# The pitch of V's rows in a cached-attention kernel: 320 bytes instead of 258

## The chip, the cores and the metric

The kernel runs on one core of one Trainium2 chip. The metric is the time of one execution on the device in microseconds (us); lower is better. The time before was 189.4 us, the median of three runs (189.28 to 189.42). All runs in this document are in the fast state (the clock is not held back), with a granted TensorE clock of 0.997 to 1.000 of full speed.

The profile names the engines PE (matmuls of TensorE), PEld (weight loads of TensorE), DVE (VectorE), ACT (ScalarE), POOL (GpSimd) and SP (SyncE, which issues most of the DMA transfers). SBUF is the on-chip memory in which the tiles lie.

## The reference, cut to what matters

```
B, Sq, D = 8, 32, 1024
Hq, Hkv, Sk, Dh = 32, 4, 8192, 128        # W = 2048 keys are used
q = (x @ wq)                              # to heads
k = k_cache[:, :, Sk - W:, :]             # each K/V head serves 8 query heads
v = v_cache[:, :, Sk - W:, :]
p = softmax(q @ k.T * Dh ** -0.5)
out = (p @ v) @ wo
```

There are 8 × 4 = 32 units, one for each batch row and K/V head. A unit has 2048 keys, cut into 16 blocks of 128, and 8 heads × 32 = 256 queries.

## The kernel before

For each unit the kernel makes scores with keys on the partitions (K is the stationary operand), takes the exponential on ACT without a maximum, and multiplies the result, P, by V; these last matmuls are called PV below. V gets a column of ones, so that the softmax sum comes out as column 129 of the same matmul. A landing buffer is a tile into which a DMA load writes. The parts that matter here:

```
self.VW = self.Dh + 1                                                     # 129
self.va = [self.c1.tile([P, self.KT, self.VW], BF16, name=f"va{i}") for i in range(3)]
# ... after it, in the same part of SBUF, lie the landing buffers of wq, wo, K and V
def va_copy(self, ui):                    # once per unit, on DVE
    self.nc.vector.tensor_copy(out=self.va[ui % 3][:, :, 0:self.Dh], in_=self.v_sb[ui][:, :, :])

for c in range(NCH):                      # 4 chunks of 4 key blocks in a unit
    for jj in range(CJ):                  # scores: 4 matmuls of 256 columns
        nc.tensor.matmul(s_ps[:, jj, :], lhsT=self.kT[ui][:, c * CJ + jj, :], rhs=q_u, ...)
    nc.scalar.activation(out=pT[:, :, :], in_=s_ps[:, :, :], func=ACT.Exp, ...)
    def pv(...):                          # run two chunks later: 8 matmuls of 129 columns
        for jj in range(CJ):
            j = c * CJ + jj
            for qt in range(QT_N):        # two halves of the queries
                nc.tensor.matmul(o_ps[:, qt, 0:self.VW], lhsT=pT[:, jj, qt * P:(qt + 1) * P], rhs=va[:, j, :], ...)
    # ... pieces of the projections and K transposes fill the rest of the slot
```

So the moving operand of PV is row j of `va`, 129 bf16 elements at j × 258 bytes, streamed twice in a row. In "a group of four rows" below, a group is one chunk: eight PV matmuls, rows 0, 0, 1, 1, 2, 2, 3, 3, preceded by the score matmuls in 126 of the 128 groups.

## Time and profile before

| | before |
|---|---|
| time, median of 3 | 189.4 us |
| PE busy | 181.3 us, 96% |
| ACT, DVE, POOL busy | 70%, 61%, 50% |
| mean step of PV matmuls (start to next start) | 57.9 ns |
| load rate between 12 and 27 us | 409 GB/s |

The page of the profile, part 1 (busy time of each engine) and the three PV groups of part 5 (busy us, mean ns of one, idle time before):

```profile
PE 181.3 (96%) x2048; PEld 154.5 (82%) x2064; DVE 115.2 (61%) x267; ACT 131.9 (70%) x133; POOL 94.2 (50%) x150
...
L473 PE MATMUL o_ps<-va_112,pT 128*128 128x129 bf16 x352 | 27.5, 220 | 0.0
L473 PE MATMUL o_ps<-va_113,pT 128*128 128x129 bf16 x352 | 27.3, 220 | 0.1
L473 PE MATMUL o_ps<-va_114,pT 128*128 128x129 bf16 x320 | 25.0, 220 | 0.0
```

PV keeps TensorE for 27.5 + 27.3 + 25.0 = 79.8 us. The 220 ns of one matmul say little: matmuls overlap (the next one starts 57.9 ns later on average), and what counts is the time from one start to the next. Those steps are not a line of any view; they are differences of the start times in the trace's matmul records. The start times of the eight PV matmuls of one group near 95 us, in us, and the steps between them in ns:

```
before: row      0       0       1       1       2       2       3       3
start        95.073  95.130  95.187  95.247  95.303  95.363  95.419  95.478
step to next     57      57      60      56      60      56      59      56
```

The first row has even steps of 57 ns; in rows 1, 2 and 3 the step after the first streaming is 59 to 61 ns, 384 times in the trace (12 rows × 32 units) without exception.

The view of waits (engine, line and tile, released by what: us in total, times, longest), the lines that matter:

```profile
ACT pT L464 <- PE s_ps L462: 35.5, 99, 1.2
...
PEld L462 <- POOL kTv L255: 1.0, 1, 1.0
...
PEld L269 <- DMA wq_sb<-in_wq_dram: 1.0, 1, 1.0
...
PEld L230 <- DMA k_raw<-in_k_cache_dram: 0.5, 1, 0.5
```

ACT waits for TensorE. TensorE waits after its start for three things: a K load at 24 us, a K that POOL transposes at 38 us, and a wq load at 63 us. After 63 us it waits for no load.

### The profile page before, as it was taken

To read this page: it belongs to the slowest core of one execution; us is meant where nothing else is said; L and a number is where in the kernel's file an instruction comes from. 1 tells how busy PE (TensorE), PEld (TensorE's weight loads), DVE (VectorE), ACT (ScalarE), POOL (GpSimd) and SP (SyncE) were. 2 spreads that over 40 slices of the span, in tenths; PEclk is the share of its full clock that TensorE was granted. 3 is DMA by queue.
4 is the path that set the end of the run, shared out by engine and by line. 5 is a ranking of instruction groups with operands and counts; after the bars stand their busy time and mean duration, and the time that the engine had idled before them with its cause. 6 is when DMAs were issued, how large, how long until landed. Compare 5 with 4: busy or idle time off the path is not lost. (4 is left out here: it accounts for less than half of the span.)

```text
span 188.6 us, 5054 instructions
## 1 busy us (share of the span) xinstructions
PE 181.3 (96%) x2048; PEld 154.5 (82%) x2064; DVE 115.2 (61%) x267; ACT 131.9 (70%) x133; POOL 94.2 (50%) x150
## 2 busy tenths in 40 slices
PE   7999999989999899999999999999999999999993
PEld 2889989979999799987878899987787888888842
DVE  0137889994595485487367648756755865355272
ACT  2218889767789687878787686787777888888700
POOL 2000004959929939947963990697199279600000
DMA  4999999999999999999899999989999899960012
GB/s 161 301 384 412 402 402 386 201 233 335 301 198 280 378 264 293 358 262 290 284 377 207 363 380 292 275 289 386 257 368 333 231 260 287 272 149 0 3 59 63
DMA packets 52507, 51.75 MB, mean 274 GB/s; under 512 B 39424, under 2 KB 40064, under 8 KB 52480
## 3 DMA queue, kind: packets, MB, share of 16 engines
q1 hardware_dynamic: 51904, 50.87, 96.3%
q10 hardware_dynamic: 576, 0.52, 0.8%
q8 instruction: 17, 0.28, 0.6%
q14 instruction: 10, 0.08, 0.1%
HBM read 41.42 MB, written 0.52 MB: 222 GB/s over the span
## 5 line engine op out<-in xcount | busy, mean ns | idle before, releaser
L464 ACT ACTIVATE pT<-s_ps 128x1024 bf16<-128x1024 f32 x128 | 129.0, 1025 | 36.5 <-PE s_ps L462 35.5
L255 POOL TENSOR_SCALAR kTv<-kb 32x512 bf16<-32x512 bf16 x140 | 93.3, 666 | 68.7 <-PE o_ps L473 29.0
L473 PEld LDWEIGHTS <-pT 128*128 128x128 bf16 x1024 | 69.3, 98 | 3.1
L462 PEld LDWEIGHTS <-kT 128*128 128x128 bf16 x368 | 34.8, 98 | 10.3
L289 PE MATMUL op_ps<-wo_sb,OT 128*128 128x512 bf16 (+1 forms) x120 | 32.9, 365 | 0.8
L269 PE MATMUL q_ps<-xT,wq_sb 128*128 128x256 bf16 x192 | 28.3, 273 | 0.7 <-DMA wq_sb<-in_wq_dram 0.7
L473 PE MATMUL o_ps<-va_112,pT 128*128 128x129 bf16 x352 | 27.5, 220 | 0.0
L473 PE MATMUL o_ps<-va_113,pT 128*128 128x129 bf16 x352 | 27.3, 220 | 0.1
L473 PE MATMUL o_ps<-va_114,pT 128*128 128x129 bf16 x320 | 25.0, 220 | 0.0
L245 DVE STREAM_TRANSPOSE kb<-k_raw 128x512 bf16<-128x512 bf16 x36 | 23.9, 685 | 0.0
L411 DVE RECIPROCAL RL_all<-o_ps 128x2 f32<-128x2 f32 x32 | 5.3, 166 | 29.5 <-PE o_ps L473 29.2
L416 DVE TENSOR_SCALAR o_sb<-o_ps,RL_all 128x128 bf16<-128x128 f32 x64 | 19.5, 347 | 1.1
L462 PEld LDWEIGHTS <-kTv 128*128 128x128 bf16 x144 | 13.8, 98 | 6.1 <-POOL kTv L255 1.0
L269 PEld LDWEIGHTS <-wq_sb 128*128 128x128 bf16 x192 | 16.9, 98 | 2.1 <-DMA wq_sb<-in_wq_dram 1.0
L462 PE MATMUL s_ps<-QT_63,kT 128*128 128x256 bf16 x112 | 16.8, 273 | 0.0
L418 DVE STREAM_TRANSPOSE OT<-o_sb 128x256 bf16<-128x256 bf16 x32 | 14.3, 445 | 1.1
L462 PE MATMUL s_ps<-QT_66,kT 128*128 128x256 bf16 x96 | 14.4, 273 | 0.1
L289 PEld LDWEIGHTS <-OT 128*128 128x128 bf16 x136 | 11.1, 97 | 2.8 <-DVEq L76 0.6
L462 PE MATMUL s_ps<-QT_65,kT 128*128 128x256 bf16 x80 | 12.0, 273 | 0.1
L462 PE MATMUL s_ps<-QT_64,kT 128*128 128x256 bf16 x80 | 12.0, 272 | 0.1
L296 DVE TENSOR_TENSOR oacc<-op_ps,oacc 128x512 f32<-128x512 f32 x8 | 5.5, 682 | 7.5 <-PE op_ps L289 7.5
L405 DVE COPY va_113<-v_sb 128x2048 bf16<-128x2048 bf16 x11 | 9.0, 820 | 0.0
(46 smaller groups left out, 105.6 us busy)
## 6 DMA issues: line engine op xcount, KB each, us to landing
v_sb<-in_v_cache_dram SPq DMA_DIRECT2D x32, 512.0 KB, 7.3
wo_sb<-in_wo_dram SPq DMA_DIRECT2D x16, 512.0 KB, 6.7
wq_sb<-in_wq_dram SPq DMA_DIRECT2D x14, 512.0 KB, 7.5
k_raw<-in_k_cache_dram SPq DMA_DIRECT2D x13, 512.0 KB, 7.2
wq_sb<-in_wq_dram SPq DMA_DIRECT2D x4, 256.0 KB, 6.6
kT<-in_k_cache_dram SPq DMA_TRANSPOSE x36, 7.1
k_raw<-in_k_cache_dram SPq DMA_DIRECT2D x2, 256.0 KB, 7.9
x_sb<-in_x_dram ACTq DMA_DIRECT2D x1, 256.0 KB, 3.8
```

What stands on the lines that cost most here:

```text
L245: nc.vector.transpose(out=st["kb"][:, sl, :], in_=self.k_raw[ui][:, sl, :])
L255: nc.gpsimd.tensor_scalar(out=out, in0=in_, scalar1=1.0, scalar2=1.0, op0=ALU.mult, op1=ALU.mult)
L269: nc.tensor.matmul(st["ps"][:, 0:self.NQ], lhsT=self.wq_t[g, i][:, c % (DC // 2), hl * P:(hl + 1) * P], rhs=self.xT[:, c, :], start=(c == ...
L289: nc.tensor.matmul(ps[:, 0:w], lhsT=self.OT[:, gq, c, t * P:(t + 1) * P], rhs=self.wo_t[gq][:, c, n0:n0 + w], start=(k == 0), stop=(k == 7))
L296: nc.vector.tensor_tensor(out=acc, in0=ps[:, 0:w], in1=acc, op=ALU.add)
L405: self.nc.vector.tensor_copy(out=self.va[ui % 3][:, :, 0:self.Dh], in_=self.v_sb[ui][:, :, :])
L411: nc.vector.reciprocal(out=rl[:, ui * QT_N:(ui + 1) * QT_N], in_=o_ps[:, :, Dh])
L416: nc.vector.tensor_scalar(out=o_sb[:, qt, :, :], in0=o_ps[:, qt, 0:Dh].rearrange("p (i c) -> p c i", c=4), scalar1=rl[:, ui * QT_N + qt:ui ...
L418: nc.vector.transpose(out=self.OT[:, g * QT_N:(g + 1) * QT_N, :, b * self.Sq:(b + 1) * self.Sq], in_=o_sb[:, :, :, :])
L462: nc.tensor.matmul(s_ps[:, jj, :], lhsT=self.kT[ui][:, c * CJ + jj, :], rhs=q_u, start=True, stop=True)
L464: nc.scalar.activation(out=pT[:, :, :], in_=s_ps[:, :, :], func=ACT.Exp, bias=0.0, scale=self.scale)
L473: nc.tensor.matmul(o_ps[:, qt, 0:self.VW], lhsT=pT[:, jj, qt * P:(qt + 1) * P], rhs=va[:, j, :], start=(j == 0 and qt == 0), stop=(j == KT ...
```

## The change

The row pitch of `va` becomes 160 elements, 320 bytes, a multiple of 64. The number of columns that PV streams stays 129.

```
+VA_ROW = 160
-        self.va = [self.c1.tile([P, self.KT, self.VW], BF16, name=f"va{i}") for i in range(3)]
+        self.va = [self.c1.tile([P, self.KT, VA_ROW], BF16, name=f"va{i}") for i in range(3)]
...
-  nc.tensor.matmul(o_ps[:, qt, 0:self.VW], lhsT=..., rhs=va[:, j, :],
+  nc.tensor.matmul(o_ps[:, qt, 0:self.VW], lhsT=..., rhs=va[:, j, 0:self.VW],
```

The intent is that each row starts at an aligned address. A side effect is not in the diff: `va` grows by 3 × 992 = 2976 bytes per partition, and all that is allocated after it moves by that much. In the built program the first landing buffer of the weights goes from address 75872 to 78848, and the K and V buffers likewise. The order of instructions on every engine is the same in both kernels.

More of the change, by code (lines that the diff above doesn't have):

```diff
@@ L472, in pv @@
                         for qt in range(QT_N):
-                            nc.tensor.matmul(o_ps[:, qt, 0:self.VW], lhsT=pT[:, jj, qt * P:(qt + 1) * P], rhs=va[:, j, :],
+                            nc.tensor.matmul(o_ps[:, qt, 0:self.VW], lhsT=pT[:, jj, qt * P:(qt + 1) * P], rhs=va[:, j, 0:self.VW],
                                              start=(j == 0 and qt == 0), stop=(j == KT - 1), skip_group_check=True)
```

## The prediction

> **What bounds the kernel.** TensorE. The page gives PE 96% busy; that is not PE at its peak, so I used start times of consecutive matmuls in the trace: score matmuls (256 columns) follow each other every 109 ns, PV matmuls (129 columns) every 57.9 ns on average. From 63 to 180 us these streams stand back to back. ACT waits 35.5 us in total for scores (the view of waits); DVE is 61% and POOL 50% busy. Before 63 us TensorE has stalls that are not its own: the start-up (about 12 us, on loads), 0.5 us on a K load at 24 us, 1.0 us on a POOL-made K at 38 us, 1.0 us on a wq load at 63 us.
>
> **What the change does.** It removes and adds no instruction; the order on every engine is the same. It changes the addresses of three tiles and of all allocated after them.
>
> 1. *The moving operand of PV.* Row j starts at 258·j bytes now, at 320·j afterwards. Each row is streamed twice (two halves of the queries). The start-to-start time after the first of the pair is 56.7 ns for j = 0, 4, 8, 12 (258·j a multiple of 8) and 60.2 ns for the other twelve, never under 59; after the second it is 56.6 and 55.9 ns. One group in the last unit has no other matmul before it, and its first row still shows 56 ns, so I read this as a cost of the row's start address, not of the place in the group. With 320-byte rows all should show 56.6 ns. Saving (estimate): 12 rows × 32 units × (60.2 + 55.9 − 2 × 56.6) = 384 × 2.8 ns = 1.1 us. [...]
>
> 2. *The DVE copy into these rows* (128x2048, 32 times): 654 to 690 ns without overlapping POOL work, up to 1092 ns with it. I expect no change; it is off the critical path anyway.
>
> 3. *Later tiles* move by 2976 bytes: landing buffers of K, V and weights, 32 bytes off a multiple of 64 before, now start on one. If that speeds loads, the stalls before 63 us shrink; this trace has no evidence[...].
>
> **On the critical path.** After 63 us 720 of the 1024 PV matmuls remain: 0.76 us of the 1.1 us go straight to the end time. The 0.3 us saved earlier run into load waits and are partly lost. ACT (1025 ns per 1.3 us of TensorE work) and POOL have slack for a TensorE 0.7% faster.
>
> **Prediction.** 189.4 − 0.9 − 0.2 = 188.3 us; 8 in 10 between 187.3 and 189.3. Faster by over 2%: 0.03; within 2%: 0.95; slower by over 2%: 0.02.
>
> **What would show it.** Step 1 right: 56 to 57 ns for every PV row, none at 60; MATMUL durations alike (now about 222 ns for shifted rows, 220 for j = 0). Wrong: the 60 ns stays at the second to fourth row of each group of four; then it is the place, not the address. Step 2: copy minimum still near 655 ns. Step 3: landing times (median about 7 us) and the stalls at 24, 38 and 63 us unchanged. ACT's wait for scores falls by about 1 us; no new wait.
>
> **What would make it wrong.** [...] faster loads could remove the early stalls (up to 2.5 us better); or the time saved could turn into waits for POOL-made K.

The sum: 189.4 us less 0.9 us for the rows, which rests on the measured steps, and less 0.2 us for the moved buffers. The 0.2 us was worked out from no measurement; without it the sum comes to 188.5 us.

## The result, and the profile after

188.31 us, the median of six runs (187.87 to 188.78), against 189.41 us for the kernel before (six runs). The ratio is 0.9947, with a 95% interval of 0.9923 to 0.9971. Ratios here are the mean time of one kernel's fast runs over that of the other's of the same rounds, so not quite the ratio of the medians. The kernel is 0.5% faster, at the predicted 188.3 us.

The same lines of the page, after:

```profile
PE 179.0 (96%) x2048; PEld 152.9 (82%) x2064; DVE 116.0 (62%) x267; ACT 131.8 (71%) x133; POOL 94.2 (51%) x150
...
L474 PE MATMUL o_ps<-va_112,pT 128*128 128x129 bf16 x352 | 27.1, 220 | 0.0
L474 PE MATMUL o_ps<-va_113,pT 128*128 128x129 bf16 x352 | 27.0, 220 | 0.1
L474 PE MATMUL o_ps<-va_114,pT 128*128 128x129 bf16 x320 | 24.7, 220 | 0.0
```

PV is now 27.1 + 27.0 + 24.7 = 78.8 us: 1.0 us less. The starts of the same group:

```
after: row       0       0       1       1       2       2       3       3
start        93.418  93.474  93.531  93.588  93.644  93.701  93.758  93.814
step to next     56      57      57      56      57      57      56      57
```

No step in the whole trace is over 57 ns where one PV matmul follows another. Over these 897 steps the sum fell from 51.98 to 50.83 us, the mean from 57.9 to 56.7 ns.

The view of waits, after:

```profile
ACT pT L465 <- PE s_ps L463: 33.2, 98, 1.3
...
PEld L463 <- POOL kTv L256: 1.1, 1, 1.1
```

The waits for the K load at 24 us and for the wq load at 63 us are gone; the one for POOL's K is still there, 0.1 us longer. Whether the moved buffers did that, or chance, is taken up in run 3. The windows view shows the side of the loads. Its columns are the window, then the busy us and instructions of PE, PEld, DVE, ACT and POOL, then the clock, the DMA share and the GB/s moved. First before, then after:

```profile
12.00:27.00 15.00, 14.60 (x212) 13.59 (x209) 11.47 (x25) 10.95 (x13) 0.00 (x0) 1.00 1.03 409
```

```profile
12.00:27.00 15.00, 14.98 (x220) 14.12 (x218) 12.24 (x26) 11.43 (x13) 0.00 (x0) 1.00 1.03 415
```

From 12 to 27 us the DMA engines are busy throughout (share 1.03 in both), and they move 415 GB/s instead of 409. The profiled executions differ more than the kernels do (spans of 188.6 and 186.4 us; the profiled run of before took 190.53 us, above all its timed runs), so a difference between two profiles is no measure of the time gained. Hence the experiments.

### The profile page after: what moved, and what is told of

It reads as the page before. It is cut to its first block, busy times and chain, and to the rows that moved or that the text cites. A ratio compares the mean times of both kernels' runs of the same rounds, so it can differ in the third digit from the quotient of the medians.

```text
span 186.4 us, 5054 instructions
## 1 busy us (share of the span) xinstructions
PE 179.0 (96%) x2048; PEld 152.9 (82%) x2064; DVE 116.0 (62%) x267; ACT 131.8 (71%) x133; POOL 94.2 (51%) x150
## 5 line engine op out<-in xcount | busy, mean ns | idle before, releaser
L465 ACT ACTIVATE pT<-s_ps 128x1024 bf16<-128x1024 f32 x128 | 129.0, 1025 | 34.2 <-PE s_ps L463 33.2
L474 PEld LDWEIGHTS <-pT 128*128 128x128 bf16 x1024 | 68.5, 98 | 3.1
L474 PE MATMUL o_ps<-va_112,pT 128*128 128x129 bf16 x352 | 27.1, 220 | 0.0
L474 PE MATMUL o_ps<-va_113,pT 128*128 128x129 bf16 x352 | 27.0, 220 | 0.1
L474 PE MATMUL o_ps<-va_114,pT 128*128 128x129 bf16 x320 | 24.7, 220 | 0.0
L406 DVE COPY va_113<-v_sb 128x2048 bf16<-128x2048 bf16 x11 | 9.7, 880 | 0.0
```

## The experiments

All edits are shown against the changed kernel. An unused tile `pad` after `va` sets where the later tiles lie. "Old place" means that they moved by a multiple of 4096 bytes in all, so they lie within any 4 KB as in the kernel before. All results were correct. Each ratio is against the kernel before, run in the same rounds, five rounds each. The rounds ran on four chips, so compare ratios and not times between groups of runs.

Two questions were asked. Does the gain come from the rows or from the moved landing buffers (runs 1 to 3, 10 to 12)? And what is it in a row of 258 bytes that costs time (runs 4 to 9)? The measured steps, in ns, are the mean over all groups of the step after the first / second streaming of each row:

| rows | row 0 | row 1 | row 2 | row 3, first | mean of 897 | ratio, 95% interval |
|---|---|---|---|---|---|---|
| 258 (before) | 56.7 / 56.6 | 60.8 / 55.9 | 60.1 / 55.9 | 59.6 | 57.9 | 1 |
| 320 (after) | 56.7 / 56.6 | 56.7 / 56.7 | 56.6 / 56.7 | 56.7 | 56.7 | 0.9947 (0.9923 to 0.9971) |
| 260 | 56.7 / 56.6 | 60.8 / 55.9 | 59.2 / 55.9 | 59.4 | 57.8 | 0.9991 (0.9972 to 1.0011) |
| 264 | 56.6 / 56.7 | 60.6 / 56.1 | 55.8 / 56.0 | 60.7 | 57.5 | 0.9966 (0.9938 to 0.9995) |
| 320, all 2 bytes off | 56.5 / 57.5 | 57.3 / 57.7 | 57.5 / 57.5 | 57.4 | 57.4 | 0.9979 (0.9949 to 1.0009) |
| 322 | 56.5 / 56.8 | 56.7 / 57.5 | 59.2 / 55.7 | 56.3 | 57.0 | 0.9993 (0.9974 to 1.0012) |
| 272 (run 12) | 56.7 / 56.6 | 56.7 / 56.7 | 56.6 / 56.7 | 56.7 | 56.7 | 0.9953 (0.9931 to 0.9974) |

### Run 1: rows of 320 bytes, later tiles in their old place

```
+        self.pad = self.c1.tile([P, 560], BF16, name="pad")      # after va: 1120 bytes
```

> Rows of 320 bytes, but every tile after V moved by 4096 bytes in all, so that the landing buffers keep their place within any 4 KB (32 bytes off a multiple of 64, as before). Theory A (the row's start address costs TensorE time): all PV matmuls 56 to 57 ns apart, as in the changed kernel, and the kernel is 0.4 to 0.6% faster than before (0.8 to 1.1 us). Theory B (the gain came from the landing buffers, now on 64-byte multiples): 0 to 0.2% faster; loads as slow as before: about 402 GB/s in the third to sixth slice, v_sb landing 7.3 us in the median, TensorE waiting for a wq load near 62 us. Both parts true: PV as A says, loads as B says, 0.3 to 0.5% faster.

Measured: 188.5 us against 189.27 us, ratio 0.996 (0.9942 to 0.9979). The PV group and the loads between 12 and 27 us:

```profile
L475 PE MATMUL o_ps<-va,pT 128*128 128x129 bf16 x1024 | 78.8, 220 | 0.1
```

```profile
12.00:27.00 15.00, 14.70 (x214) 13.68 (x212) 11.56 (x25) 11.14 (x13) 0.00 (x0) 1.00 1.03 408
```

PV as in the changed kernel, loads as in the kernel before, and 0.4% of the 0.5% gained. The rows carry most of it.

### Run 2: rows of 258 bytes, later tiles where the change puts them

```
-VA_ROW = 160
+VA_ROW = 129
+        self.pad = self.c1.tile([P, 1488], BF16, name="pad")     # 2976 bytes
```

> Rows of 258 bytes as before, and an unused tile of 2976 bytes per partition after V, so that all later tiles stand at the addresses that the changed kernel gives them. Theory A: PV matmuls 57.9 ns apart on average with the 60 ns in place, time as before (within 0.1%). Theory B: loads as in the changed kernel (about 414 GB/s in slices four to six, v_sb landing near 6.4 us), no wait for wq near 62 us, 0.2 to 0.5% faster.

Measured: 189.01 us against 189.27 us, ratio 0.9987 (0.9972 to 1.0002). The PV group of the page, and the window from 12 to 27 us:

```profile
L475 PE MATMUL o_ps<-va,pT 128*128 128x129 bf16 x1024 | 79.8, 220 | 0.1
```

```profile
12.00:27.00 15.00, 15.00 (x216) 14.10 (x215) 12.12 (x26) 11.62 (x13) 0.00 (x0) 1.00 1.03 416
```

PV as before, loads as in the changed kernel: the faster loads come from where the tiles after V lie. Those tiles include the transposed K and pT, which TensorE reads, but its PV steps stay at 57.9 ns on average. V's landing was expected near 6.4 us in the median and was 6.9, against 7.0 in the control (run 3): that time is no good marker. Of their worth the timed runs say only that it is small: the interval reaches to no gain at all.

### Run 3: the control

```
-VA_ROW = 160
+VA_ROW = 129
+        self.pad = self.c1.tile([P, 2048], BF16, name="pad")     # 4096 bytes
```

> A control: rows of 258 bytes and an unused tile of 4096 bytes, so that later tiles move but keep their place within any 4 KB. Both theories: as before within 0.1%, PV 57.9 ns, v_sb landing near 7.3 us, early waits on loads as before. If the loads come as fast as in the changed kernel or the early waits are gone here, they differ from run to run by chance, and B has no ground.

Measured: 189.51 us against 189.27 us, ratio 1.001 (0.9993 to 1.0026): a move by 4096 bytes changed nothing that the runs can tell. PV was as before, and the window from 12 to 27 us shows the loads as before:

```profile
L475 PE MATMUL o_ps<-va,pT 128*128 128x129 bf16 x1024 | 79.8, 220 | 0.1
...
12.00:27.00 15.00, 14.71 (x215) 13.85 (x213) 11.92 (x26) 11.18 (x13) 0.00 (x0) 1.00 1.03 407
```

The wait for wq near 63 us was not there in this run, although nothing that matters had changed. It comes and goes: 0.9 us in the profile of before, 0.5 us in run 8, 0.2 us in run 6, under 0.1 us in the others. So its absence after the change proves nothing. The step into the K transposes at 24 us is another matter. Of the eleven profiles with buffers off a multiple of 512 bytes (the kernel before among them), TensorE lost 0.37 to 0.71 us there in seven, 0.21 us in run 6, 0.17 us in run 8 and nothing in runs 5 and 7; in the three with buffers on a multiple (after, run 2, run 11) it lost 0 to 0.15 us. That fits faster loads, but it is no proof either.

### Run 4: rows of 260 bytes

```
-VA_ROW = 160
+VA_ROW = 130
+        self.pad = self.c1.tile([P, 2000], BF16, name="pad")     # old place
```

> Rows of 260 bytes (even rows start on a multiple of 8, odd rows 4 bytes off), later tiles in their old place within 4 KB. Theory A (address, multiples of 8): about 60 ns after the first matmul of the pair for j odd only, 56 to 57 ns for j even; PV 57.3 ns on average. Rival (place in the group of four rows): 60 ns for the second, third and fourth row of each group, as before, 57.9 ns on average. If 4 bytes suffice: all 56.6 ns. Time 0.2 to 0.3% faster under A, as before under the rival.

Measured: 188.98 us against 189.27 us, ratio 0.9991. Row 2 starts at 520 bytes, a multiple of 8, and still shows 59.2 ns. So the prediction's reading, that a start on a multiple of 8 is free, was wrong. By this run alone the rival (the place in the group) held. But two of my observations speak against it: rows of 320 bytes have no slow place, and in the kernel before, one group in the last unit follows another PV group directly and its first row is fast. That row, row 8, starts at 8 × 258 = 2064 bytes, a multiple of 16. This gave theory C: count the addresses in blocks of 16 bytes; a row pays when it begins in the block in which the row streamed just before it ended. The size can be worked out from the two traces, if C has the right form. Row 2 here begins at byte 520 and row 1 ends at byte 517: no block of 8 bytes holds both, yet row 2 took 59.2 ns. Row 8 of the kernel before begins at byte 2064 and row 7 ends at 2063: a block of 32 bytes holds both, yet row 8 took 56 ns, in the one group that shows it. Of the powers of two that leaves 16. The expectations call such a block a line; no run shows that it is a unit of the memory. After score matmuls, whose operand lies elsewhere, the first row of a group pays nothing (56.7 ns here and before).

### Run 5: rows of 264 bytes

```
-VA_ROW = 160
+VA_ROW = 132
+        self.pad = self.c1.tile([P, 1904], BF16, name="pad")     # old place
```

> Rows of 264 bytes (all on multiples of 8, odd rows 8 bytes off a multiple of 16), later tiles in their old place within 4 KB. The run with 260-byte rows has shown 60 ns for rows 1, 2 and 3 of each group, row 2 on a multiple of 8 included, so my reading of the address alone has failed. Theory C (a row pays when its first bytes lie in the same 16-byte line as the last bytes of the row streamed just before it): 60 ns for odd rows alone, 56 to 57 for even ones, PV 57.3 ns on average. Theory A (multiples of 8 suffice): 56.6 for all; already doubtful. Shared lines of 32 or 64 bytes: rows 1, 2 and 3 of each group at 60. Place in the group: rows 1, 2 and 3 at 60. Time under C: 0.2 to 0.3% faster than before.

Measured: 188.95 us against 189.44 us, ratio 0.9966. Odd rows, 8 bytes off a multiple of 16, show 60.6 and 60.7 ns; even rows show 55.8 ns. This is what C says with blocks of 16 bytes. By itself it fits another rule as well: a row pays when it starts further into its 16-byte block than the row before did (call it G; runs 8 and 9 bear on it). It excludes the place in the group, 8 bytes as enough, and shared blocks of 32 or 64 bytes, which would have slowed row 2.

### Run 6: rows of 320 bytes, all 2 bytes off

```
-  rhs=va[:, j, 0:self.VW]            # and likewise in the copy and in the memset of ones
+  rhs=va[:, j, 1:1+self.VW]
+        self.pad = self.c1.tile([P, 560], BF16, name="pad")      # old place
```

> Rows of 320 bytes with V one element (2 bytes) into each row: every row starts 2 bytes off a multiple of 16, and no row shares a line with its neighbour. Theory C (shared line with the row before): no 60 ns at all, PV 56.6 ns, 0.4% faster than before, like rows of 320 bytes alone. Theory D (a start off a multiple of 16 costs, wherever the row before ended, except after a score matmul): 60 ns for rows 1, 2 and 3 of each group, 57.9 ns on average, time as before.

Measured: 189.15 us against 189.44 us, ratio 0.9979. Not one step of 60 ns: a start 2 bytes off a multiple of 16 does not by itself cost 4 ns, and theory D falls. But the steps are 57.5 ns instead of 56.7, in second streamings too. So here a start 2 bytes off has a small price of its own, 0.8 ns, that C does not contain. It is not a price of every unaligned start: rows 4 and 12 of the kernel before start 8 bytes off a multiple of 16, and their steps average 56.5 to 56.8 ns.

### Run 7: the two query halves in the outer loop

```
-VA_ROW = 160
+VA_ROW = 129
+        self.pad = self.c1.tile([P, 2048], BF16, name="pad")     # old place
-                    for jj in range(CJ):
-                        j = c * CJ + jj
-                        for qt in range(QT_N):
+                    for qt in range(QT_N):
+                        for jj in range(CJ):
+                            j = c * CJ + jj
```

> Rows of 258 bytes in their old place, but the two query halves in the outer loop: rows 0, 1, 2, 3 for the first half, then 0, 1, 2, 3 for the second; the same matmuls. Theory C: now six of eight steps go from a row to its neighbour instead of three, so 60 ns stand after rows 1, 2, 3 of both halves; PV (2 x 56.6 + 6 x 60)/8 = 59.2 ns on average, if each costs as much as it does now, and 0.4 to 0.6% slower than before. Theory E (streaming the same unaligned row a second time costs): no 60 ns, 56.6 on average, 0.4% faster. Place after the scores: seven of eight at the slower step.

Measured: 190.17 us against 189.44 us, ratio 1.0034 (1.0005 to 1.0064). The steps after the eight matmuls' first seven, in ns: 56.7, 60.8, 59.2, 59.4, then in the second half 55.8, 60.2, 59.2; mean 58.8. The PV group of the page:

```profile
L475 PE MATMUL o_ps<-va,pT 128*128 128x129 bf16 x1024 | 80.9, 221 | 0.0
```

The same matmuls in another order are slower, because now six of eight go from a row to its right neighbour instead of three. The slowdown is a little under the 0.4 to 0.6% expected, as the mean step is under the 59.2 ns expected. G predicts the same steps as C here, since in this order too every row that shares a block starts further into it. The rival E, that a second streaming of the same row is what costs, predicted the opposite sign and falls.

### Run 8: rows in the order 0, 2, 1, 3

```
-VA_ROW = 160
+VA_ROW = 129
+        self.pad = self.c1.tile([P, 2048], BF16, name="pad")     # old place
-                    for jj in range(CJ):
+                    for jj in (0, 2, 1, 3):
```

> Rows of 258 bytes in their old place, but the four rows of each group in the order 0, 2, 1, 3, so that no row follows its left neighbour. Theory C: no 60 ns, PV 56.6 ns, 0.4% faster than before, with no memory spent on padding. Theories A and D (the address alone) and the place in the group: 57.9 ns and the time as before.

Measured: 188.88 us against 189.44 us, ratio 0.9963 (0.9933 to 0.9992), with a mean step of 57.2 ns. C had promised 56.6 and the address-alone theories 57.9: it is in between. Row 2, which now follows row 0 and shares no block with it, has 58.2 ns in the first and third chunk of a unit and 60.0 ns in the second and fourth; row 3 after row 1 has 58.4 and 60.0 ns. Row 1 after row 2, the one step back, has 55.9 ns. So C is not the whole. G fits all three: rows 2 and 3 start further into their block than the row before, row 1 does not. The slow steps of 58 ns start 4 or 6 bytes into the block, those of 60 ns 12 or 14 bytes.

### Run 9: rows of 322 bytes

```
-VA_ROW = 160
+VA_ROW = 161
+        self.pad = self.c1.tile([P, 2560], BF16, name="pad")     # old place
```

> Rows of 322 bytes: their starts run through the same places within 16 bytes as rows of 258 bytes (0, 2, 4, 6, ...), but 64 bytes lie between a row's end and the next row's start; later tiles in their old place within 4 KB. Theory C (the first bytes lie in the same 16-byte line as the last bytes of the row before): no step over 58 ns; 57 to 57.5 ns on average, with the 0.8 ns that a start 2 bytes off has shown. Rival F (a start at another place within 16 bytes than the row before costs, wherever that row ended): 60.9, 60.1 and 59.3 ns for rows 1, 2 and 3 of a group as with 258 bytes, 57.9 on average. In between, as the order 0, 2, 1, 3 has shown (58.2 and 60): neither rule is the whole, and the document says that it stays open.

Measured: 189.16 us against 189.25 us, ratio 0.9993 (0.9974 to 1.0012). The starts run through the same places within 16 bytes as with 258, only with 64 bytes between rows, and the slow steps of rows 1 and 3 are gone (56.7 and 56.3 ns against 60.8 and 59.6). Rival F falls, and so does G as a whole, because all three rows start further into their block than the row before. But row 2 keeps 58.5 ns in the first and third chunk (4 bytes into its block) and 60.0 ns in the others (12 bytes), against what C says. The PV steps sum to 51.10 us, 0.88 us less than before, but the timed runs show hardly any gain. The wait for the K load at 24 us was the longest of all runs here (0.7 us). Against the profile of the control, run 9 is 0.45 us shorter from the 305th PV matmul (near 63 us) to the 1017th, and loses 0.3 us more at the K load. If the timed runs were like the profiled one, the 0.1 to 0.2 us that this leaves lies within the interval, which is 0.4% wide.

### Run 10: later tiles on multiples of 64 bytes

```
-VA_ROW = 160
+VA_ROW = 129
+        self.pad = self.c1.tile([P, 48], BF16, name="pad")       # 96 bytes
```

> Rows of 258 bytes, and an unused tile of 96 bytes after V: later tiles on multiples of 64 bytes, but not of 128. Theory B2 (landing on multiples of 64 is enough for faster loads): 4 KB packets between 8 and 25 us at 159.5 ns on average and slices four to six at 411 to 415 GB/s, as in the changed kernel; PV 57.9 ns; 0 to 0.2% faster than before. Theory B3 (512 bytes are needed): packets at 162 ns and 402 to 409 GB/s, as before.

Measured: 189.55 us against 189.25 us, ratio 1.0021 (0.9994 to 1.0049). The window from 12 to 27 us:

```profile
12.00:27.00 15.00, 14.70 (x213) 13.81 (x210) 11.81 (x25) 11.66 (x13) 0.00 (x0) 1.00 1.03 406
```

Loads as before: with the buffers on multiples of 64 bytes, which the prediction had named, they moved 406 GB/s. Places on multiples of 128 and 256 that are none of 512 were not tried. Over all fourteen profiles, the three kernels with buffers on multiples of 512 moved 415, 416 and 416 GB/s in this window, the eleven others 406 to 409. Packets of 4 KB between 8 and 25 us took 159.4 to 159.8 ns on average in the three and 161.4 to 162.5 ns in the others. That is what was measured with these places; why they differ is not shown.

### Runs 11 and 12: rows of 272 bytes, with and without the places

```
-VA_ROW = 160
+VA_ROW = 136
+        self.pad = self.c1.tile([P, 128], BF16, name="pad")      # run 11: 256 bytes, to a multiple of 512
+        self.pad = self.c1.tile([P, 1712], BF16, name="pad")     # run 12 instead: old place
```

> Rows of 272 bytes (multiples of 16, no shared line), and later tiles on multiples of 512 bytes by an unused tile of 256 bytes: 0.9 KB per partition spent instead of 2.9. Theory C: every PV step 56 to 57 ns, 56.7 on average, loads as in the changed kernel, 0.5% faster than before: the same as rows of 320 bytes. If 64-byte steps of the row matter: slower steps than 57 ns in rows off a multiple of 64.

> Rows of 272 bytes, later tiles in their old place within 4 KB: the run just before without its other half. If the two parts add up (rows 0.4%, places 0.1 to 0.2%): every PV step 56 to 57 ns, loads at 405 to 407 GB/s between 12 and 27 us (the run with places on multiples of 512 bytes had 414), a wait of 0.3 to 0.7 us for a K load at 24 us, and 0.3 to 0.5% faster than before. If the places alone make the gain: as before within 0.1%. If the rows alone make it: 0.6% faster, as with both.

Run 11: 188.23 us against 189.25 us, ratio 0.9938 (0.9918 to 0.9958). It does what the change does with 672 + 256 = 928 bytes per partition instead of 2976; the two are not told apart in time. Its PV group, and the window from 12 to 27 us:

```profile
L475 PE MATMUL o_ps<-va,pT 128*128 128x129 bf16 x1024 | 78.8, 220 | 0.1
```

```profile
12.00:27.00 15.00, 14.97 (x219) 14.01 (x216) 12.09 (x26) 11.29 (x13) 0.00 (x0) 1.00 1.03 416
```

Run 12: 188.33 us against 189.29 us, ratio 0.9953 (0.9931 to 0.9974). The same two lines:

```profile
L475 PE MATMUL o_ps<-va,pT 128*128 128x129 bf16 x1024 | 78.8, 220 | 0.0
...
12.00:27.00 15.00, 14.63 (x213) 13.62 (x211) 11.55 (x25) 10.95 (x13) 0.00 (x0) 1.00 1.03 407
```

With run 1 this is the second measurement of the rows alone: 0.40% and 0.47%. With the places added the ratios are 0.9947 and 0.9938, lower by 0.13 and 0.15 percentage points. Run 2 gives 0.13% for the places alone. The three agree, but each is smaller than its interval is wide, so the time that the places gain is not established; the load rate is.

## Why the prediction was right, and where it was not

*The size was right.* The prediction took 384 × 2.8 ns = 1.1 us off TensorE. The 897 steps that can be measured gave 1.15 us, and the 127 steps from a PV matmul to something else lost about 0.1 us of it (they go from 56 to 57 ns). On the path to the end it expected 0.76 us from the rows after 63 us, and 0.9 us from the rows in all. The part after 63 us can be read from the start times: from the 305th PV matmul to the 1017th, the kernel before and runs 2, 3 and 10 (rows of 258 bytes in the old order) took 114.63 to 114.65 us, and the changed kernel and runs 1, 11 and 12 (aligned rows) 113.88 to 113.89 us, wherever the later tiles lay. That is 0.75 us. The two runs with the rows alone gave 0.40% and 0.47% of 189.3 us, which is 0.76 and 0.89 us. The prediction gave the moved buffers 0.2 us in its sum; the differences above amount to 0.13% of 189.3 us, about 0.25 us, not settled. That the median came within 0.01 us of the sum is luck: the interval of the ratio is 0.9 us wide, and the 0.2 us had no evidence behind it. That the rows' term came out is not luck alone: it was the measured excess of the slow steps, and at 320 bytes the rule that was assumed (multiples of 8) and the rules that the runs suggest (below) all promise that it goes.

*The loss on the way was right in kind.* In run 1 against the control the step at 38 us, where TensorE waits for POOL's K, is 0.94 us over its work instead of 0.87 (0.94 in all four profiles with aligned rows, 0.87 to 0.90 in the four with rows of 258 bytes in the old order): of what TensorE had saved before this wait, which is not its own, 0.07 us was given back there. A second small loss was not foreseen. In 19 places scores follow PV directly, with no other piece between, and there the step grew from 59.9 to 63.6 ns, 0.07 us in all. In such a slot TensorE needs 8 × 56.7 + 4 × 109 = 890 ns and ACT 1025 ns; that TensorE there waits for ACT to free a score buffer is an inference.

*The reason given for step 1 was wrong.* The prediction said that the cost was the row's start address and that multiples of 8 were free. Rows of 260 and 264 bytes refute it. In the trace of before, the rows on multiples of 8 were also the first rows of their groups, coming after score matmuls; the one group that followed another PV group was trusted to separate the two, but its row lies on a multiple of 16 as well. Nor does the start address alone cost much: 0.8 ns when every row is 2 bytes off. What the runs show instead is that the cost depends on the row before (run 8: the same rows in another order, a mean of 57.2 ns instead of 57.9), and on places within 16 bytes. Where the rows run in order with pitches of 258, 260 and 264 bytes (before, runs 4, 5 and 7), the rows that begin in the 16-byte block in which the row streamed just before ended, and only they, take 59 to 61 ns, 2.5 to 4 ns more. How many such blocks a row touches is the same for every row, 17 at any of these pitches, and so cannot make the difference; 16 bytes is where it appears (odd rows at a pitch of 264 bytes pay, with 60.6 and 60.7 ns, no row at 272 does, with 56.6 to 56.7 ns). The prediction also read the durations of shifted rows as about 222 ns; by row they average 219.5 to 221.2 ns before, and 220 ns for every row after.

*What stays open.* In those in-order runs a row that shares a block also starts further into it than the row before, so they cannot tell C from G. Runs 8 and 9 can, and disagree: all three changes of row in run 8 fit G and only one fits C; in run 9 rows 1 and 3 fit C and row 2 fits G. Neither rule is the whole. The slow rows of runs 8 and 9 differ between chunks as their starts do (4 or 6 bytes into the block against 12 or 14), but with 258 bytes in the old order no such difference shows. Nor has any run shown what happens inside the memory. With rows on multiples of 16 (272 and 320 bytes were run, every step 56.6 to 56.7 ns on average) none of it arises, so the layout is settled and the mechanism is not.

*Step 2 was right.* The DVE copy into `va` (minimum, median and maximum of 32) took 653, 689 and 1092 ns before and 650, 684 and 1125 ns after. It gains nothing from aligned rows.

*Step 3 was half right.* Landing times were expected to stay, and the loads became 1.5 to 2% faster from 12 to 27 us (415 to 416 GB/s against 406 to 409); the median landing of V fell from 7.3 to 6.4 us between the two profiles, but hardly between runs 3 and 2 (7.0 and 6.9). Multiples of 64 bytes, of which the prediction thought, did not bring it (406 GB/s in run 10). The three kernels with the faster loads had their buffers on multiples of 512; why those places differ is not shown. Of the three stalls, the one at 24 us went (but runs 5 and 7, with the buffers in their old place, lack it too), the one at 63 us comes and goes by chance, and the one at 38 us stayed. ACT's wait for scores fell by 2.3 us between the two profiles, not 1; between run 1 and the control it fell from 34.6 to 33.8 us, which is the predicted size.

## What to carry to other kernels

Where TensorE bounds a kernel and streams one short row after the other, try rows with a pitch that is a multiple of 16 bytes; here 272 bytes did all that 320 did (a mean step of 56.7 ns at both, 57.9 at 258), and even the order of the loop moved the time by 0.3 to 0.4% with unaligned rows. A change of a tile's size moves everything allocated after it: before the gain is put down to the tile, run the old tile with the new places, and the new tile with the old places. And a pattern in one trace that fits two readings (here an address and a place in a loop) needs a layout in which the two disagree.
